# Attention and two expert layers on one core: each engine's instruction order as a written table in place of a list scheduler, with the banded scores' matmul groups of two head pairs joined

## The chip, the cores and the metric

The kernel runs on one core of one Trainium2 chip. Five engines work side by side, each on its own queue of instructions, which it takes in order: PE (TensorE, matmuls, with a separate record PEld for its weight loads), DVE (VectorE), ACT (ScalarE), POOL (GpSimd) and SP (SyncE, which here only issues DMA transfers). An instruction that waits for another engine holds up everything behind it in its own queue. The metric is the device time of one launch in microseconds (us), the median of repeated runs; less is better.

## The reference

Three stages run one after the other. The first is attention over 4 batches, 8 heads, 576 positions of 64 numbers: a full softmax attention over means of 4 neighbouring positions (144 of them), repeated 4 times, plus a banded one in which each position sees only those less than 4 places away. Then come two expert layers over the 2304 tokens of 512 numbers.

```
out_up = np.repeat(sm_attn(q_d, k_d, v_d), 4, axis=2)     # q_d: mean of 4 positions
mask = np.abs(pos[:, None] - pos[None, :]) < 4
scores = np.where(mask, scale * q @ k.T, -1e9)
attn = out_up + softmax(scores) @ v                       # (2304, 512) as x
h = x @ w_in                                              # 512 x 2048
x = (np.maximum(h, 0) + alpha * np.minimum(h, 0)) @ w_out # 2048 x 512
xn = x / np.sqrt(np.mean(x * x) + 1e-6) * rms_g
g = xn @ w_gate                                           # 512 x 1536
out = (g * sigmoid(g) * (xn @ w_val)) @ w_out2            # 1536 x 512
```

## The kernel before

All weights arrive as 64-bit floats and are turned into 32-bit ones on the chip. A piece of a weight lies raw in a tile `wr` (two 32-bit halves to a number, fetched at L1167 or L1177); `decode` (L1186 to L1195) makes it a 32-bit float in a tile `wc` (or `wo`): one ACT pass over the high halves (L1186), for some pieces a second ACT pass over the low ones (L1189) and one DVE pass (L1191), for the others two DVE passes (L1194, L1195). `square` (L1207, tile `sqps`) then lets TensorE multiply each 128-column block with itself, DVE takes the diagonal (L1208), and a sum over all partitions (L415, tile `allps`) gives the scale of that weight. With it every operand is split into a high and a low f16 half (ACT L439, DVE L440), and a product is taken as three f16 matmuls: high by high, high by low, low by high.

The 2304 tokens go through in blocks. **Attention of the first tokens and the decoding of the first weights** fill the start. Queries and keys of a pair of heads are loaded (L819, tile `wo`) and transposed (L868, tile `tps`, copied by ACT at L869 into a tile `T`), then follow the scores of the coarse attention (L891, `sps`), its transposed weights (L919, L920), its product with the values (L928), and the banded attention in chunks: mask (L944, L948), scores (L956, tile `lsps`), exponentials on ACT (L976), transposes (L1000, `ltps`, copied at L1002 into `laT`) and the product with the values (L1012, `lops`). From the output a scaled f16 pair `xt` is made. **First expert layer**: L1432 (`hps`) computes h, ACT and DVE apply the slope (L1436, L1438) and split it (L439, L440) and L1449 (`acc`) multiplies by w_out. Attention of later tokens (DVE and POOL, for some batches TensorE, L545 to L770) lies under these matmuls. **Second expert layer**: L1684 (`pa`, `pb`, `pf`) gate and value products, L1807 (`oacc`) and L1927 (`px`, `py`) the last product, L1932 the copy of the output and L1966 its transfer.

The scores of a pair of heads at L956 and the products at L1012 use a 64-row or 64-column part of TensorE's array, two heads beside each other; most other matmuls use all 128 by 128. A `tile size` below means the part that a matmul uses.

What sets the order: the program records some 9,200 instructions, and at its end `issue_order(tc, nc, groups)` decides in which order each engine takes its own. It is a list scheduler: it knows what each instruction needs, gives each a cost, the waits between engines and a rule for TensorE's two speeds, goes over the program 40 times backward and forward, and keeps the best order that it finds. The table `LEADS` then shifts ranges of instructions by some nanoseconds of priority, and one last pass gives the order, which is nailed down by dependencies between each instruction and the next. Matmuls recorded inside `with together():` form a group that nothing may come between. Each such group holds the 4 matmuls (2 positions by 2 heads) of one head pair:

```python
                for n, h in enumerate(hs):
                    T_ = self.st[h]["T"]
                    with together():
                        for i in range(QC):
                            ...
                                nc.tensor.matmul(ps[j][0:QT, n, i], T_[j * 64:j * 64 + 64, 0, q0:q0 + QT],
```

Of the kernel before, what the change touches and what calls it, by code (L numbers as in the profile page):

```python
# [18 lines left out]
def view(ap, dims, off=0, parts=None):  # L19
# [4 lines left out]
LEADS = (  # L24
# [43 lines left out]
)  # L68


def issue_order(tc, nc, groups, rounds=40):


    insts = [i for i in nc.cur_bb.bb.instructions if i.opcode != "TilePoolBoundary"]
    count = range(len(insts))
    eng = [str(i.engine).split(".")[-1] for i in insts]
    ring, slots = {}, {}
    for t in tc.info.tiles:
        ring.setdefault(t.tag, []).append(t.name)
        slots[t.name] = t.bufs or t.tag_meta.bufs  # L80

    def free(a):
        n = 1
        for _, c in list(a.ap)[1:]:
            n *= c
        return n

    def row(a):
        n = 1
        for d in a.tensor.shape[1:]:  # L90
            n *= d
        return n

    def wide(a):
        return 2 if "16" in str(a.dtype) else 4

    def psum(a):
        return "PSUM" in str(a.tensor.space)

    def span(a):  # L100
        if psum(a):
            return 0, 128, 0, 1 << 20
        p, lo = divmod(a.offset, row(a))
        hi = lo + 1 + sum(abs(s) * (n - 1) for s, n in list(a.ap)[1:])
        return p, p + a.ap[0][1], lo * wide(a), hi * wide(a)

    def meets(x, y):
        return x[0] < y[1] and y[0] < x[1] and x[2] < y[3] and y[2] < x[3]

    def covers(x, y):  # L110
        return x[0] <= y[0] and x[1] >= y[1] and x[2] <= y[2] and x[3] >= y[3]

    def runs(a):
        dims = [list(d) for d in a.ap]
        n, length = 1, 1
        for step, c in reversed(dims):
            if c == 1:
                continue
            if step == length and (n == 1):
                length *= c  # L120
            else:
                n *= c
        return n, length

    def transfer(o, i):
        sides = [[c for _, c in a.ap if c > 1] or [1] for a in (o, i)]
        rings = max(x for x in range(1, 17) if not any(s[0] % x for s in sides))
        n = max(runs(a)[0] for a in (o, i))
        each = 4.0 * min(runs(a)[1] for a in (o, i))
        share = n / 16 * (10.0 + 0.046 * each)  # L130
        return max(share, n / rings * (9.0 + 0.042 * each)), max(share, 600.0)

    def cost(k, ins, outs):
        i, e = insts[k], eng[k]
        if not outs:
            return 60.0
        o, n = outs[0], free(outs[0])
        if e == "SP":
            return transfer(o, ins[0])[0]
        if e == "PE":  # L140
            if wide(ins[0]) == 2:
                return max(25.0, n / 2.4 + 2.5)
            return n * 2 / 2.4 + 3 if i.is_transpose else n * 4 / 2.4 + (128 if n < 64 else 8)
        n = max([n] + [free(a) for a in ins[:1]])
        extra = len([a for a in ins[1:] if free(a) == 1 and n > 1])
        if e == "Activation":
            return (61 if psum(ins[0]) else 103) + n / 1.2 + 93 * (extra + len(outs) - 1)
        if e == "DVE":
            if i.opcode == "Reciprocal":
                return 89 + 6.25 * n  # L150
# [32 lines left out]
    users = {}  # L183
# [136 lines left out]
def kernel(  # L320
# [31 lines left out]
    W = 3  # L352
# [1779 lines left out]
```

## Time and profile before

| | us |
|---|---|
| median of 3 runs | 912.55 (912.38 to 913.46) |
| the profiled execution | 912.48 |
| its span in the trace | 910.8 |
| PE busy | 885.3 (97% of the span) |
| DVE, ACT, POOL busy | 729.8, 570.0, 401.8 |

The profiled execution is within 0.1 us of the median, and its span lies 1.7 us below its own time; what is outside the span is the launch. Busy times are those of the trace and add up to more than the span, since the engines overlap.

### The profile page before, as it was taken

To read this page: it belongs to the slowest core of one execution; us is meant where nothing else is said; L and a number is where in the kernel's file an instruction comes from. 1 tells how busy PE (TensorE), PEld (TensorE's weight loads), DVE (VectorE), ACT (ScalarE), POOL (GpSimd) and SP (SyncE) were. 2 spreads that over 40 slices of the span, in tenths; PEclk is the share of its full clock that TensorE was granted. 3 is DMA by queue.
4 is the path that set the end of the run, shared out by engine and by line. 5 is a ranking of instruction groups with operands and counts; after the bars stand their busy time and mean duration, and the time that the engine had idled before them with its cause. 6 is when DMAs were issued, how large, how long until landed. Compare 5 with 4: busy or idle time off the path is not lost.

```text
span 910.8 us, 16778 instructions
## 1 busy us (share of the span) xinstructions
PE 885.3 (97%) x6394; PEld 592.8 (65%) x6394; DVE 729.8 (80%) x1358; ACT 570.0 (63%) x1332; POOL 401.8 (44%) x314
## 2 busy tenths in 40 slices
PE   7987999999999999999999999999999999999997
PEld 5766877799866666666666656654566644556686
DVE  4789987799898788798789789999899891288772
ACT  5999986255763366765796688983366641356730
POOL 1100204999899999496201233211623100268630
PEclk9998999999999999999999999999999999999999
DMA  9976351174333141340630002220000001100001
GB/s 224 297 261 209 104 182 28 53 234 142 106 89 99 44 95 53 102 139 1 195 87 32 1 1 81 94 70 35 24 13 1 1 1 39 32 1 1 1 19 53
DMA packets 54111, 73.81 MB, mean 81 GB/s; under 512 B 22202, under 2 KB 35918, under 8 KB 54030
## 3 DMA queue, kind: packets, MB, share of 16 engines
q1 hardware_dynamic: 54030, 72.74, 26.7%
q8 instruction: 50, 0.82, 0.4%
q14 instruction: 31, 0.25, 0.1%
HBM read 68.01 MB, written 4.72 MB: 80 GB/s over the span
## 4 chain that ended last, share of the span: by engine, by line
PE 85%; ACT 6%; DVE 3%; DMA 2%; POOL 2%; issue 1%; SPq 0%; DVEq 0%; POOLq 0%; ACTq 0%
PE hps L1432 18%; PE acc L1449 17%; PE pa L1684 14%; PE oacc L1807 10%; PE pf L1684 7%; PE pb L1684 3%; PE px L1927 3%; POOL prod L599 1%; PE py L1927 1%; PE lsps L956 1%; PE tps L868 1%; ACT wr L1186 1%; PE lops L1012 1%; ACT wi L439 1%; PE ltps L1000 1%
## 5 line engine op out<-in xcount | busy, mean ns | idle before, releaser
L1432 PE MATMUL hps<-xt,wi 128*128 128x192 f16 (+1 forms) x1536 | 326.8, 290 | 4.6 <-DVE g L440 3.1
L1449 PE MATMUL acc<-ghl,wo 128*128 128x384 f16 (+1 forms) x960 | 231.0, 310 | 0.0
L1432 PEld LDWEIGHTS <-wi 128*128 128x128 f16 x1536 | 148.6, 100 | 57.1 <-issue 6.5
L1449 PEld LDWEIGHTS <-wo 128*128 128x128 f16 x1344 | 128.4, 98 | 56.7 <-issue 0.8
L545 POOL TENSOR_TENSOR prod<-cq,ckv 128x896 f32<-128x896 f32 x48 | 105.5, 2197 | 41.4 <-DVE hps L1438 35.3
L1684 PEld LDWEIGHTS <-ws 128*128 128x128 f16 x864 | 85.0, 99 | 56.7 <-issue 2.7
L599 POOL TENSOR_TENSOR prod<-ls,ckv 128x896 f32<-128x896 f32 x48 | 91.3, 1903 | 9.8 <-DVE lo L612 6.5
L1807 PE MATMUL oacc<-wi,wo 128*128 128x512 f16 x360 | 95.4, 379 | 0.2 <-ACT ob L1811 0.2
L1684 PEld LDWEIGHTS <-w 128*128 128x128 f16 x648 | 63.8, 99 | 41.6 <-issue 0.5
L1436 ACT ACTIVATE g<-hps 128x384 f32<-128x384 f32 x96 | 47.2, 492 | 61.5 <-PE hps L1432 60.9
L1438 DVE SCALAR_TENSOR_TENSOR hps<-g,oma,hps 128x192 f32<-128x192 f32 (+1 forms) x128 | 65.7, 515 | 18.3 <-ACT g L1436 17.3
L1449 PE MATMUL acc<-g,wo 128*128 128x384 f16 (+1 forms) x384 | 70.3, 286 | 0.1
L1664 POOL TENSOR_TENSOR ws<-w 128x768 f32<-128x768 f16 x12 | 22.1, 1852 | 106.8 <-DVE ws L1571 40.8
L1684 PE MATMUL pa<-x,w 128*128 128x384 f16 x216 | 67.1, 326 | 0.1
L1684 PE MATMUL pb<-x,w 128*128 128x384 f16 x216 | 66.2, 326 | 0.0
L1807 PEld LDWEIGHTS <-wo 128*128 128x128 f16 x360 | 35.3, 98 | 41.8 <-issue 0.5
L439 ACT ACTIVATE ghl<-hps,grp 128x384 f16<-128x384 f32 (+1 forms) x73 | 42.2, 578 | 31.9 <-DVE hps L1438 27.2
L612 DVE TENSOR_REDUCE lo<-prod 128x128 f32<-128x896 f32 x48 | 51.7, 1079 | 9.5 <-POOL prod L599 9.2
L1692 DVE TENSOR_TENSOR sn<-pf,sn 128x384 f32<-128x384 f32 x45 | 24.8, 552 | 42.6 <-ACT sn L1689 36.5
L556 DVE TENSOR_REDUCE ls<-prod 128x14 f32<-128x896 f32 x48 | 51.7, 1078 | 4.6 <-POOL prod L545 4.5
L1689 ACT ACTIVATE sn<-pa 128x384 f32<-128x384 f32 x66 | 31.9, 489 | 32.9 <-PE pa L1684 32.7
L1876 POOL TENSOR_TENSOR wr<-wi 128x512 f32<-128x512 f16 x12 | 15.1, 1261 | 84.1 <-DMA out_dram<-ob 77.5
(365 smaller groups left out, 2122.6 us busy)
## 6 DMA issues: line engine op xcount, KB each, us to landing
wr<-in_moe_w_out_dram SPq DMA_DIRECT2D x18, 512.0 KB
wr<-in_moe_w_in_dram SPq DMA_DIRECT2D x10, 768.0 KB
wr<-in_moe_w_gate_dram SPq DMA_DIRECT2D x8, 768.0 KB
wr<-in_moe_w_val_dram SPq DMA_DIRECT2D x8, 768.0 KB
ckv<-in_k_dram SPq DMA_DIRECT2D x7, 768.0 KB
ckv<-in_v_dram SPq DMA_DIRECT2D x7, 768.0 KB
wr<-in_moe_w_out_dram SPq DMA_DIRECT2D x20, 256.0 KB
out_dram<-ob SPq DMA_DIRECT2D x14, 256.0 KB
```

Source lines behind the costliest of these rows:

```text
L439: nc.scalar.activation(out=hi, in_=src, func=AF.Copy, scale=s)
L545: engs[i].tensor_tensor(out=pr, in0=view(st["q"][:, j, t:t + TP], [[D, TP], [0, ND], [1, D]]), in1=view(st["k"][:, j, t:t + TP], [[D, TP], ...
L556: nc.vector.tensor_reduce(out=st["s"][:, j, t:t + TP], in_=st.pop(("p", i)), axis=AX.X, op=ALU.add)
L599: engs[i].tensor_tensor(out=over(pr, i), in0=view(st["s"][:, j, t:t + TP], [[ND, TP], [1, ND], [0, D]]), in1=view(st["v"][:, j, t:t + TP], ...
L612: nc.vector.tensor_reduce(out=st["o"][:, t:t + TP, j], in_=view(pr, [[ND * D, TP], [ND, D], [1, ND]]), axis=AX.X, op=ALU.add)
L1432: nc.tensor.matmul(ps[:, j], wi[:, f + j, a, kk * 128:(kk + 1) * 128], x[:, b_, kk, c0:c0 + n], start=(i == 0), stop=(i == 3 * KK - 1))
L1436: nc.scalar.activation(out=g, in_=ps, func=AF.Relu, scale=-1.0)
L1438: nc.vector.scalar_tensor_tensor(out=ps[:, j], in0=g[:, j], scalar=oma[:, f + j:f + j + 1], in1=ps[:, j], op0=ALU.mult, op1=ALU.add)
L1449: nc.tensor.matmul(acc[e], wo_f(f)[:, a, e * 128:(e + 1) * 128], hl[:, b_], start=(f == f0 and i == 0), stop=(f == f1 and i == 2))
L1684: nc.tensor.matmul(ps, w[:, a, kk, c:c + 128], x[:, b_, kk], start=(start and n == 0), stop=(n == 3 * K2 - 1), skip_group_check=True)
L1807: nc.tensor.matmul(acc, uhl(f)[:, h, a, tt * 128:(tt + 1) * 128], w[:, b_, f % 3], start=(f == fs[0] and i == 0), stop=(f == fs[-1] and i ...
L1927: nc.tensor.matmul(ps, two(u[g])[:, a, tt * 128:(tt + 1) * 128], w(g, b_), start=(start and g == 0 and i == 0), stop=(g == F2 - 1 and i == 2),
```

## The change

The scheduler, its costs, the `LEADS` and the groups go. In their place stands `ORDER`, a table with one list for each engine; each number is the step from one instruction's place in the program to that of the next. The matmuls, the other work and the transfers are the same 9,181 instructions of data work as before, and only their order on each engine differs. No line is kept that holds the four matmuls of a group together; the table decides it.

```diff
-LEADS = (
-    (8102, 8103, 7000), (776, 777, -500), (3486, 3544, 1500), (7335, 7386, 500), (5591, 5593, -500),
...
-def issue_order(tc, nc, groups, rounds=40):
...
+ORDER = {
+    "Activation": (
+        127, -4, 13, -4, 9, 4, 285, 1, -281, 17, -2, 1, -12, 14, 64, 2, 2, -3, 5, -3, 2, -52, 54, 194, -184, -1, 3,
...
+def issue_order(tc, nc):
+    insts = [i for i in nc.cur_bb.bb.instructions if i.opcode != "TilePoolBoundary"]
...
+    for engine, steps in ORDER.items():
+        k, a = 0, None
+        for step in steps:
+            k += step
+            b = insts[k]
...
+            if a is not None:
+                tc.add_manual_dep(b, a.name, wait if apart(a) else info, reason="issue order")
+            a = b
...
-                    with together():
-                        for i in range(QC):
-                            q0 = W + (c * QC + i) * QT
-                            for j in range(2):
...
+                    for i in range(QC):
+                        q0 = W + (c * QC + i) * QT
+                        for j in range(2):
...
-    issue_order(tc, nc, groups)
+    issue_order(tc, nc)
```

How that moves rows is seen in the order of each engine. A row names the line, the operation, what it writes and reads, its shape, and with x how many stand in a row. After the change lines lie 117 to 121 further down (L956 is L1074, L1432 is L1549, L1186 is L1303).

TensorE, where the banded scores of the third chunk of the first tokens stand among the first layer's matmuls (`T_186` and `T_191` are the transposed queries and keys of two head pairs). Before:

```order
L948 MATMUL lsps<-maskb 96x2x3
L1432 LDWEIGHTS wi
L1432 MATMUL hps<-xt,wi 128x192
L956 MATMUL lsps<-T_186 96x102 x4
L1432 LDWEIGHTS wi
L1432 MATMUL hps<-xt,wi 128x192
L956 MATMUL lsps<-T_191 96x102 x4
L1432 LDWEIGHTS wi
L1432 MATMUL hps<-xt,wi 128x192
L733 MATMUL sps<-qkT 72x144 x4
L1000 MATMUL ltps<-ident,dls 102x96
```

The same place with the change:

```order
L1549 LDWEIGHTS wi
L1549 MATMUL hps<-xt,wi 128x192
L1074 MATMUL lsps<-T_186 96x102 x4
L1074 MATMUL lsps<-T_191 96x102 x4
L855 MATMUL sps<-qkT 72x144 x4
L1118 MATMUL ltps<-ident,dls 102x96
L1549 LDWEIGHTS wi
L1549 MATMUL hps<-xt,wi 128x192
```

The groups of the two head pairs stand next to each other now, and the coarse scores, which use half the array too, behind them, where a matmul of the full array stood between each two before. In the whole program L956 stood in 16 runs of four; now in six runs of eight and four of four. From the first `hps` matmul on, the tile size changes 89 times along TensorE's order, and changed 100 times before.

ACT, from the last copies of `laT` of the first chunk to the first split of w_in (`wi`) and the first slope (`g`). Before:

```order
L1002 ACTIVATE laT<-ltps 102x384
L1186 ACTIVATE wr<-wr 128x768
L439 ACTIVATE xt<-dxs,sc 128x192
L1186 ACTIVATE wr<-wr 128x768
L439 ACTIVATE xt<-dxs,sc 128x192
L1189 ACTIVATE wr<-wr,nhalf 128x768
L1186 ACTIVATE wr<-wr 128x768
L1189 ACTIVATE wr<-wr,nhalf 128x768
L1186 ACTIVATE wr<-wr 128x768
L439 ACTIVATE wi<-wc,swi 128x512 x5
```

With the change:

```order
L1303 ACTIVATE wr<-wr 128x768
L1120 ACTIVATE laT<-ltps 102x384
L1306 ACTIVATE wr<-wr,nhalf 128x768
L1120 ACTIVATE laT<-ltps 102x384
L1303 ACTIVATE wr<-wr 128x768
L562 ACTIVATE xt<-dxs,sc 128x192
L1306 ACTIVATE wr<-wr,nhalf 128x768
L562 ACTIVATE xt<-dxs,sc 128x192
L562 ACTIVATE wi<-wc,swi 128x512 x2
L1303 ACTIVATE wr<-wr 128x768
L562 ACTIVATE wi<-wc,swi 128x512 x3
```

Behind the last `laT` stood four L1186, two L1189 and two `xt` before the first `wi`; now one L1303 (the same line), one L1306 (L1189) and two `xt` do. The others stand ahead of `laT`, but for one L1186 that comes after the first `wi`. Counted from the program's start, 13 of L1186 preceded the first `wi`, and 12 do now; all else ahead of it is the same.

SP, from the program's start, the first loads. Before (the rows of two small vectors are `rows`, a piece of w_in is `wr`):

```order
L819 DMA wo<-in_q_dram 96x6x64
L1167 DMA wr<-in_moe_w_in_dram 128x2x768
L819 DMA wo<-in_q_dram 96x6x64
L819 DMA wo<-in_k_dram 96x6x64
L2031 DMA rows<-in_moe_alpha_dram 16x128
L827 DMA sdv<-in_v_dram 72x2x512
L2031 DMA rows<-in_moe_rms_g_dram 4x128
```

With the change:

```order
L940 DMA wo<-in_q_dram 96x6x64
L2148 DMA rows<-in_moe_alpha_dram 16x128
L940 DMA wo<-in_k_dram 96x6x64
L940 DMA wo<-in_q_dram 96x6x64
L2148 DMA rows<-in_moe_rms_g_dram 4x128
L940 DMA wo<-in_k_dram 96x6x64
L940 DMA wo<-in_q_dram 96x6x64
L1284 DMA wr<-in_moe_w_in_dram 128x2x768
```

The first of these rows is the seventh transfer before and the fifth with the change. The two small rows went from the eleventh and thirteenth place to the sixth and ninth, the first piece of w_in from the eighth to the twelfth, behind two loads of q and k and the two small rows that followed it before. On TensorE the two transposes that read the small rows (L2034, `vecps`) follow their transfers: they stand behind the fifth and the eighth transpose L868 now, and stood behind the seventeenth and the twenty-third.

## Rows read from the trace of the kernel before

**Rows 1.** The page, busy time of each engine (part 1) and the chain (part 4).

```profile
PE 885.3 (97%) x6394; PEld 592.8 (65%) x6394; DVE 729.8 (80%) x1358; ACT 570.0 (63%) x1332; POOL 401.8 (44%) x314
...
PE 85%; ACT 6%; DVE 3%; DMA 2%; POOL 2%; issue 1%; SPq 0%; DVEq 0%; POOLq 0%; ACTq 0%
```

**Rows 2.** Windows: the span cut into stretches, busy time of each engine, granted clock.

```profile
0.00:10.00 10.00, 3.52 (x18) 2.76 (x20) 1.85 (x10) 2.73 (x5) 2.06 (x27) 1.00 0.93 201
10.00:50.00 40.00, 40.00 (x278) 31.04 (x279) 28.89 (x84) 36.35 (x123) 4.84 (x4) 1.00 0.95 267
50.00:60.00 10.00, 8.14 (x67) 6.60 (x66) 9.16 (x25) 8.58 (x14) 0.00 (x0) 1.00 0.72 237
60.00:92.00 32.00, 24.27 (x242) 21.22 (x244) 30.13 (x74) 31.67 (x78) 2.13 (x2) 0.89 0.73 236
92.00:99.00 7.00, 7.00 (x92) 5.66 (x90) 6.57 (x22) 4.79 (x16) 1.97 (x6) 1.00 0.48 132
99.00:905.00 806.00, 802.27 (x5714) 525.54 (x5708) 652.24 (x1145) 485.86 (x1101) 390.82 (x275) 1.00 0.20 62
905.00:911.00 6.00, 0.10 (x1) 0.00 (x0) 1.01 (x3) 0.00 (x0) 0.00 (x0) 0.93 0.24 82
```

**Rows 3.** Chain of waits inside 50 to 93 us: start, length, what.

```profile
57.63 6.66 DMA wr<-in_moe_w_in_dram
...
64.31 0.94 ACT wr L1186
...
91.76 0.55 PE lops L1012 x8
```

**Rows 4.** Waits of ACT, 10 to 92 us: total, times, longest.

```profile
ACT T L869 <- PE tps L868: 1.4, 3, 0.8
ACT aT L920 <- PE atps L919: 1.1, 2, 0.6
ACT laT L1002 <- PE ltps L1000: 0.9, 1, 0.9
ACT wr L1186 <- DMA wr<-in_moe_w_in_dram: 0.8, 2, 0.5
ACT wi L439 <- DVE swi L430: 0.5, 1, 0.5
```

**Rows 5.** Timeline of TensorE: start, length, line, operation, tiles, shapes, count, idle before.

```profile
6.80 1.19 PE L868 MATMUL tps<-ident,wo 96*128 96x96 f32 x6 [3.31 <-DMA wo<-in_q_dram]
8.33 1.22 PE L868 MATMUL tps<-ident,wo 96*128 96x96 f32 x6 [0.34 <-ACT T L869]
...
33.28 1.55 PE L1012 MATMUL lops<-laT,vw 102*64 102x96 f32 x16
34.78 0.76 PE L891 MATMUL sps<-qkp 64*72 64x144 f32 x4
...
50.60 0.91 PE L1012 MATMUL lops<-laT,vw 102*64 102x96 f32 x8
51.44 0.40 PE L1000 MATMUL ltps<-ident,dls 96*102 96x96 f32 x1
```

**Rows 6.** The same view, runs of the first layer's matmuls, and the banded scores among them.

```profile
60.80 2.42 PE L1432 MATMUL hps<-xt,wi 128*128 128x192 f16 x14 [0.40 <-DVE wi L440]
...
64.40 1.81 PE L1432 MATMUL hps<-xt,wi 128*128 128x192 f16 x20
...
94.81 0.24 PE L1432 MATMUL hps<-xt,wi 128*128 128x192 f16 x1
94.98 0.60 PE L956 MATMUL lsps<-T 64*96 64x102 f32 x8
95.51 0.26 PE L1432 MATMUL hps<-xt,wi 128*128 128x192 f16 x1
```

**Rows 7.** Waits of PE, 99 to 905 us.

```profile
PE pa L1684 <- ACT sn L1689: 1.6, 3, 0.8
PE atps L761 <- ACT dd L752: 1.0, 1, 1.0
```

More of the change, by code (lines that the diff above doesn't have):

```diff
@@ L1 @@
-import heapq
 from collections import deque
-from contextlib import ExitStack, contextmanager
+from contextlib import ExitStack
 import concourse.bass as bass
@@ L312, in issue_order, with apart @@
+ORDER = {
+    "Activation": (
[51 rows of a table added]
+    ),
+    "DVE": (
[60 rows of a table added]
+    ),
[255 rows of a table added]
+    ),
+    "Pool": (
[13 rows of a table added]
+    ),
[12 rows of a table added]
+    ),
+}
+def issue_order(tc, nc):
+    insts = [i for i in nc.cur_bb.bb.instructions if i.opcode != "TilePoolBoundary"]
     info, wait = [mybir.DependencyInfo(c, mybir.DependencyReason.DATA)
                   for c in (mybir.DependencyClass.NoSync, mybir.DependencyClass.Sync)]
-    for q in best[1].values():
-        for a, b in zip(q, q[1:]):
-            tc.add_manual_dep(insts[b], insts[a].name, wait if apart[a] else info, reason="issue order")
+    def apart(i):
+        outs = [a.bass_ap for a in i.outs if hasattr(a, "bass_ap")]
+        return str(i.engine).endswith("Pool") and outs and outs[0].tensor.name.split("_")[0] in ("prod", "sd", "qkp", "dd")
+    placed = 0
+    for engine, steps in ORDER.items():
[3 more added lines that the diff above has]
+            b = insts[k]
+            assert str(b.engine).split(".")[-1] == engine
+            if a is not None:
+                tc.add_manual_dep(b, a.name, wait if apart(a) else info, reason="issue order")
+            a = b
+            placed += 1
+    assert placed == len(insts)
@@ L357 @@
     P_X, P_W, P_H = 13, 14, 15
-    groups = []
-    @contextmanager
-    def together():
-        n = len(nc.cur_bb.bb.instructions)
-        yield
-        groups.append([i.name for i in nc.cur_bb.bb.instructions[n:]])
     P_N, P_U, P_G, P_O = 8, 38, 13, 13
@@ L729, in smm @@
             ps = [ps_t.tile([128, 2, SD], F32, tag="at", name="sps") for j in range(2)]
-            with together():
-                for a in range(2):
-                    for j in range(2):
-                        nc.tensor.matmul(
-                            ps[j][0:SH, a], t[j * 64:j * 64 + 64, 0, a * SH:(a + 1) * SH],
-                            t[j * 64:j * 64 + 64, 1, :], start=True, stop=True)
+            for a in range(2):
+                for j in range(2):
+                    nc.tensor.matmul(
+                        ps[j][0:SH, a], t[j * 64:j * 64 + 64, 0, a * SH:(a + 1) * SH],
+                        t[j * 64:j * 64 + 64, 1, :], start=True, stop=True)
             a_ = st["buf"][:, 0:4 * SD].rearrange("p (j a k) -> p j a k", j=2, a=2)
@@ L769, in avm @@
             ps = ps_t.tile([128, SD], F32, tag="at", name="avps")
-            with together():
-                for kh in range(2):
-                    for j in range(2):
-                        nc.tensor.matmul(ps[j * 64:j * 64 + 64, :], st["pv"][:, kh, j],
-                                         st["aT"][:, j, kh * SD:(kh + 1) * SD], start=(kh == 0), stop=(kh == 1))
+            for kh in range(2):
+                for j in range(2):
+                    nc.tensor.matmul(ps[j * 64:j * 64 + 64, :], st["pv"][:, kh, j],
+                                     st["aT"][:, j, kh * SD:(kh + 1) * SD], start=(kh == 0), stop=(kh == 1))
             nc.scalar.activation(out=outd_t[b][:, h, :], in_=ps, func=AF.Copy)
@@ L887, in smm @@
                 ps = [pool_of(self.smp[j]).tile([128, 2, SD], F32, tag=self.smp[j], name="sps") for j in range(2)]
-                with together():
-                    for a in range(2):
-                        for j in range(2):
-                            nc.tensor.matmul(
-                                ps[j][0:SH, a], t[j * 64:j * 64 + 64, 0, a * SH:(a + 1) * SH],
-                                t[j * 64:j * 64 + 64, 1, :], start=True, stop=True)
+                for a in range(2):
+                    for j in range(2):
+                        nc.tensor.matmul(
+                            ps[j][0:SH, a], t[j * 64:j * 64 + 64, 0, a * SH:(a + 1) * SH],
+                            t[j * 64:j * 64 + 64, 1, :], start=True, stop=True)
                 m = att.tile([SH, 2, 2], F32, tag=f"dm{h % 2}", name="dm")
@@ L924, in avm @@
                 ps = ps_t.tile([128, SD], F32, tag="at", name="avps")
-                with together():
-                    for kh in range(2):
-                        for j in range(2):
-                            nc.tensor.matmul(ps[j * 64:j * 64 + 64, :], st["pv"][:, j, kh],
-                                             st["aT"][:, j, kh * SD:(kh + 1) * SD], start=(kh == 0), stop=(kh == 1))
+                for kh in range(2):
+                    for j in range(2):
+                        nc.tensor.matmul(ps[j * 64:j * 64 + 64, :], st["pv"][:, j, kh],
+                                         st["aT"][:, j, kh * SD:(kh + 1) * SD], start=(kh == 0), stop=(kh == 1))
                 if h == 0:
@@ L951, in s1 @@
                     T_ = self.st[h]["T"]
-                    with together():
-                        for i in range(QC):
-                            q0 = W + (c * QC + i) * QT
-                            for j in range(2):
-                                nc.tensor.matmul(ps[j][0:QT, n, i], T_[j * 64:j * 64 + 64, 0, q0:q0 + QT],
-                                                 T_[j * 64:j * 64 + 64, 1, q0 - W:q0 + QT + W],
-                                                 start=False, stop=(n == 1 and i == QC - 1))
+                    for i in range(QC):
+                        q0 = W + (c * QC + i) * QT
+                        for j in range(2):
+                            nc.tensor.matmul(ps[j][0:QT, n, i], T_[j * 64:j * 64 + 64, 0, q0:q0 + QT],
+                                             T_[j * 64:j * 64 + 64, 1, q0 - W:q0 + QT + W],
+                                             start=False, stop=(n == 1 and i == QC - 1))
                 m = att.tile([QT, 2, QC, 2], F32, tag=f"lm{h0}", name="dlm")
@@ L1008, in s4 @@
                     ps = pool_of(banks[n]).tile([128, QC, QT], F32, tag=banks[n], name="lops")
-                    with together():
-                        for i in range(QC):
-                            for j in range(2):
-                                nc.tensor.matmul(ps[j * 64:j * 64 + 64, i], st["vw"][:, c * QC + i, j],
-                                                 ls["t"][n][:, i, j], start=True, stop=True)
+                    for i in range(QC):
+                        for j in range(2):
+                            nc.tensor.matmul(ps[j * 64:j * 64 + 64, i], st["vw"][:, c * QC + i, j],
+                                             ls["t"][n][:, i, j], start=True, stop=True)
                     tag = ("ob", "xs", "ra", "rb")[h]
```

218 lines of the change are left out of this document (removed), and 432 rows, old and new, of tables (LEADS, ORDER).

## Prediction

> **What bounds the kernel now.** I read the page first: TensorE is busy for 885.3 of 910.8 us and holds 85% of the chain [rows 1]. An order can shorten the rest, or make TensorE's own work shorter, and nothing else. The windows then say where the rest lies [rows 2]. TensorE is idle for 6.5 us of the first 10 (10.00 less 3.52), for none of the 40 to 50 us, for 1.9 us from 50 to 60, for 7.7 from 60 to 92, for none from 92 to 99, for 3.7 from 99 to 905 (806.00 less 802.27) and for 5.9 in the tail; together 25.7. So there are three regimes. Up to 92 us the start, in which ACT is the fullest engine: 36.35 of 40, 8.58 of 10, 31.67 of 32 us. From 92 to 905 us TensorE, full to within 3.7 us. Then the copy and the transfer of the output.
>
> The chain inside the start shows the hand-over [rows 3]: from a transfer of w_in, 57.63 us, through ACT's decoding from 64.31 us on to TensorE's `lops` at 91.76 us, after which TensorE doesn't wait any more for ACT. Whatever ACT's own work is, it must be done before; only ACT's idle time ahead of that point can be won there. The list of ACT's waits from 10 to 92 us gives 1.4 us for `T`, 1.1 for `aT`, 0.9 for `laT`, 0.8 for transfers and 0.5 for the scale `swi` [rows 4], 4.7 together.
>
> TensorE runs the start at two speeds. Eight small `lops` matmuls took from 50.60 to 51.44 us, 0.84, and 0.55 at 91.76 us with the last one's end in it [rows 3, 5]; fourteen `hps` at 60.80 us took 2.42 us (0.17 each) and twenty at 64.40 us 1.81 us (0.09 each) [rows 6]. That is the step from 1.2 to 2.4 GHz, in the middle of the first layer's first matmuls. The granted clock is 0.89 on the mean from 60 to 92 us, so some 22% of that stretch, 7 us, is at the lower level again; from 99 us on it is 1.00 [rows 2].
>
> **The change, term by term.** All sums stand against the profiled execution, 912.48 us; the median is 0.07 above it, which I leave out.
>
> *The hand-over from ACT to TensorE.* The same work stands ahead of the first layer, but for one decode (L1186, 0.94 us in [rows 3]) that moves behind the first `wi`; it must still be done before 91 us, so I count nothing for it. What moves the hand-over is ACT's idle time. Two decodes that stood behind the last `laT` now stand ahead of it, so ACT has something to do where it waited 0.9 us for `ltps`: -0.9. The decodes on which the scale hangs are earlier, so the wait of 0.5 us for `swi` goes: -0.5. The loads of q and k pass the first 768 KB piece of w_in, so the transposes of the second pair of heads and their `T` copies can come earlier; that wait is 1.4 us, and ACT used part of the time before for the decode that is now later, so I take half: -0.7. Against it, the two small rows' transposes stand ahead of the first transposes of k. TensorE takes its queue in order, so these k transposes and the `T` copies behind them wait for two more transfers. The price isn't in the trace; from below it is nothing, from above 1.5 us, the distance between the first q and the first k transposes (6.80 and 8.33 us, [rows 5]), and I take 0.5, nearer to nothing since these rows are small and were issued early: +0.5. Sum -1.6, with the bounds -4.7 (all of ACT's idle time goes) and +1.5 (nothing goes, and the small rows cost all they can).
>
> *Joined groups and fewer changes of tile size.* In the saturated part every saved nanosecond of TensorE counts. From `hps` at 94.81 to the scores at 94.98 us lie 0.17 us, where `hps` to `hps` takes 0.09 [rows 6]: 0.08 to get in. What it costs to get out I read from the products L1012: sixteen in one run took 34.78 less 33.28, 1.50 us, and eight took 0.84 [rows 5], so two runs of eight 1.68, 0.18 more at the lower clock; half of that, 0.09, at the upper. A join saves one way in and one out, 0.17 us. Four of the six joins lie in the part that TensorE bounds: -0.7. All 11 changes of tile size that go after the first `hps` would give 11 x 0.085 = 0.9. I take the latter, -0.9, since the coarse scores and others moved together too; the bounds are nothing (the engine behind a group was waited for anyway) and -1.0.
>
> *The waits from 99 to 905 us.* There are 3.7 us to win and no limit to what may be lost. The two largest are `pa` for ACT's `sn`, 1.6 us in three waits, and `atps` for `dd`, 1.0 in one [rows 7]. The new order takes the matmuls of the second layer in shorter turns: L1684 in 201 runs where there were 120, L1807 in 118 for 67. Shorter turns put more other work between a matmul and what it needs, and also more products of different tiles in flight. I count 0, with -3.7 and +4 as bounds, the latter five waits like the longest `pa` one (0.8).
>
> *The tail.* The last matmuls, the two copies of the output and its transfer keep their order; the 5.9 us stay.
>
> **Sum:** 912.48 - 1.6 - 0.9 = 910.0 us.
>
> **Rivals.** *The clock rises earlier or falls less (faster).* In the new order the squares before the first `hps` stand together more purely, with the small products L1012 behind them, and TensorE's waits between 60 and 92 us, 7.7 us, may lie elsewhere. If the 7 us at the lower level were run at the upper, the work in them would take half, 3.5 us less; against it, the lower level lies in a stretch that ACT bounds, so TensorE's speed there only counts where ACT waits for it. With the forecast's terms that gives 912.48 - 2.5 - 3.5 = 906.5 us. The Trainium skill (TensorE: Matmul & The Clock Gate, Part 1 and Part 4) says that activity releases the lower rate and that transposes on TensorE don't count as activity in the same way. The trace agrees with the first half only in part, since TensorE was busy for 40 of 40 us from 10 to 50 and still took 0.84 us for eight products at 50.60.
>
> *The order makes new waits in the saturated part (slower).* A table that is right for one set of durations has no slack where a duration is another: TensorE waits at the head of its queue, with all matmuls behind it. The place is the second layer, `pa` on ACT's `sn`, where the three waits of before are 0.5 us each [rows 7] and turns are shorter now. It decides from 4.3 us of new waits on (2.5 for the terms above and 1.8 for the bound of what can be measured), eight or nine such waits among the 201 turns; with ten, 5.3 us, the time is 915.3. Against it: ACT is busy for 485.86 of 806 us there and DVE for 652.24 [rows 2], so both have room.
>
> *The order does what it says and nothing is won.* ACT's idle time moves to other waits, since the same decodes and transfers must be done before 91 us, and the tile changes lie under other latencies. Then it is 912 us, some tenths either way. For it speaks that ACT is busy for 31.67 of 32 us from 60 on, whatever the order.
>
> **How the numbers follow.** The forecast (two terms, 908.5 to 910.7) gets 0.37, the earlier clock 0.20, no gain 0.25, new waits 0.18. I predict the likeliest, 910.0 us. A measurement of this kernel tells about 0.2%, 1.8 us, from no change: faster by more than that are the first two, 0.57, same 0.25, slower 0.18. The range drops a tenth at either end: below, the clock's case with the larger bound of the first term on top of it (905.5), above, new waits of about 4.5 us with no gain elsewhere half kept (915.0).
>
> **What would show each step.** First term: the chain hands over to TensorE before 91 us, and ACT's waits from 10 to 92 us come to less than 4.7, with none for `swi` and `laT`; the first `hps` lies near 58 us. If the small rows cost, the first k transposes start later than 8.33 us. Second: the joined scores in one row of sixteen matmul passes with 1.1 us or less, and TensorE's busy time from 99 on smaller by under 1 us. Third: the waits of TensorE after 99 us near 3.7. Tail: 5.9 us. The prediction is wrong if the waits after 99 us are over 6, if the stretch to 92 us ends more than 4 us earlier, or if the granted clock before 92 us is another.

## The result, and the profile after

The changed kernel is slower by half a percent: 917.91 us (median of 6 runs, 916.20 to 921.90) against 912.87 us of the kernel before on the same chip, a ratio of 1.0051 with a 95% interval of 1.0027 to 1.0075. The forecast was 910.0 us, and its range ended at 915.0.

The page of the profiled execution, whose span is 917.2 us, with the busy times and the chain by engine that answer to [rows 1]:

```profile
PE 882.2 (96%) x6394; PEld 590.5 (64%) x6394; DVE 729.3 (80%) x1358; ACT 567.6 (62%) x1332; POOL 404.6 (44%) x314
...
PE 76%; ACT 6%; POOL 6%; DVE 5%; DMA 3%; SPq 2%; issue 1%; DVEq 0%; POOLq 0%; ACTq 0%
```

TensorE is busy for 3 us less, and the span is 6.4 us longer. GpSimd's share of the chain rose from 2% to 6%. The windows tell where, in the stretches of [rows 2] from 10 us on; the columns are as there:

```profile
10.00:50.00 40.00, 33.38 (x229) 25.75 (x228) 26.19 (x71) 31.59 (x102) 5.76 (x8) 1.00 0.92 247
50.00:60.00 10.00, 7.19 (x55) 5.83 (x56) 5.37 (x15) 6.41 (x26) 2.71 (x1) 1.00 0.81 255
60.00:92.00 32.00, 22.38 (x220) 19.10 (x218) 29.87 (x70) 31.03 (x53) 0.00 (x0) 0.88 0.70 221
92.00:99.00 7.00, 6.85 (x73) 6.48 (x73) 6.14 (x24) 5.83 (x25) 1.69 (x2) 0.81 0.59 161
99.00:905.00 806.00, 802.07 (x5747) 525.28 (x5745) 656.15 (x1166) 490.20 (x1128) 392.60 (x283) 1.00 0.21 62
```

From 99 to 905 us nothing changed: 3.9 us of idle TensorE, 3.7 before. The loss is in the start. TensorE was busy for all 40 us from 10 to 50 and is now for 33.38; ACT, which bounds the start, for 31.59 instead of 36.35 there, and for 6.41 instead of 8.58 from 50 to 60. The first layer's first matmul shows what the start lost; before, and with the change:

```profile
59.91 0.50 PE L1432 MATMUL hps<-xt,wi 128*128 128x192 f16 x2 [0.82 <-ACT wi L439]
...
66.54 0.26 PE L1549 MATMUL hps<-xt,wi 128*128 128x192 f16 x1 [1.26 <-ACT wi L562]
```

It comes 6.6 us later, and the span is 6.4 us longer. The list of ACT's waits from 10 to 92 us, which answers to [rows 4] (5.2 us over the whole list then, with two small rows that [rows 4] leaves out, 12.7 now), names three places:

```profile
ACT aT L1040 <- PE atps L1039: 4.8, 2, 3.6
ACT T L990 <- PE tps L989: 3.7, 5, 1.7
ACT wr L1303 <- DMA wr<-in_moe_w_in_dram: 2.6, 2, 2.2
```

The first is followed back with GpSimd's timeline. `dd` is its multiplication of the coarse attention's weights by the reciprocals of their sums; the four of the first tokens are the same work, 72 by 576 numbers each. The third and the fourth:

```profile
41.94 1.14 POOL L1029 TENSOR_TENSOR dd<-dd,dsum 72x576 f32<-72x576 f32 x1 [8.06 <-DVE dsum L1028]
47.94 4.76 POOL L1029 TENSOR_TENSOR dd<-dd,dsum 72x576 f32<-72x576 f32 x1 [4.86 <-ACT dls L1094]
```

The first three take 1.14 us each, the fourth 4.76. In VectorE's timeline over the same time stands a chain of six instructions without a gap, from 48.16 us until 51.70: four of decodes, a split and a short reciprocal.

```profile
48.16 0.55 DVE L1311 TENSOR_SCALAR wc<-wr 128x768 int32<-128x768 int32 x1
48.62 1.82 DVE L1312 SCALAR_TENSOR_TENSOR wc<-wr,wc 128x768 int32<-128x768 int32 x2
50.36 0.41 DVE L563 SCALAR_TENSOR_TENSOR xt<-dxs,sc,xt 128x192 f16<-128x192 f32 x1
50.69 0.15 DVE L558 RECIPROCAL sc<-sc 128x1 f32<-128x1 f32 x1
50.77 0.94 DVE L1308 SCALAR_TENSOR_TENSOR wo<-wr 128x768 int32<-128x768 int32 x1
```

The `dd` ends 1.0 us after the last of them, 52.70 us, about as long as it takes alone. TensorE's transposes `atps` wait for it, and ACT's copy `aT` waits 3.6 us behind that (above):

```profile
PE atps L1039 <- POOL dd L1029: 3.5, 1, 3.5
```

The Trainium skill (SBUF — State Buffer, Who interferes with whom) says that VectorE and GpSimd share a pair of ports as an exclusive lock, which a VectorE instruction with two inputs from the SBUF, or in a two-port mode, holds for its whole length, and that who issues first decides. The trace agrees on the first: 3.6 us of standstill beside that chain. It goes beyond it, since GpSimd was kept out for a chain of six instructions and not for one, and it differs on who comes first, as the last section tells.

The second and third wait belong to transfers, at least in their largest parts. The first decode of w_in begins at 14.77 us (10.50 before), after ACT has waited 2.2 us. On TensorE the transposes of a k piece begin at 25.78 us after 3.23 us of idle time; the last part of that piece landed at 25.69 us.

### The profile page after: what moved, and what is told of

The parts are those of the page before. It is cut to its first block, busy times and chain, and to the rows that moved or that the text cites. A ratio compares the mean times of both kernels' runs of the same rounds, so it can differ in the third digit from the quotient of the medians.

```text
span 917.2 us, 16746 instructions
## 1 busy us (share of the span) xinstructions
PE 882.2 (96%) x6394; PEld 590.5 (64%) x6394; DVE 729.3 (80%) x1358; ACT 567.6 (62%) x1332; POOL 404.6 (44%) x314
## 4 chain that ended last, share of the span: by engine, by line
PE 76%; ACT 6%; POOL 6%; DVE 5%; DMA 3%; SPq 2%; issue 1%; DVEq 0%; POOLq 0%; ACTq 0%
PE acc L1566 16%; PE hps L1549 15%; PE pa L1801 14%; PE oacc L1924 9%; PE pf L1801 7%; PE pb L1801 4%; PE px L2044 3%; POOL prod L722 3%; POOL prod L668 2%; DMA sdv<-in_v_dram 1%; PE py L2044 1%; DMA wr<-in_moe_w_out_dram 1%; ACT wr L1303 1%; SPq L940 1%; DVE lo L735 1%
## 5 line engine op out<-in xcount | busy, mean ns | idle before, releaser
L1549 PE MATMUL hps<-xt,wi 128*128 128x192 f16 (+1 forms) x1536 | 326.9, 289 | 7.2 <-DVE g L563 4.2
L1566 PE MATMUL acc<-ghl,wo 128*128 128x384 f16 (+1 forms) x960 | 228.4, 310 | 0.0
L1549 PEld LDWEIGHTS <-wi 128*128 128x128 f16 x1536 | 147.2, 100 | 58.2 <-issue 4.4
L1924 PE MATMUL oacc<-wi,wo 128*128 128x512 f16 x360 | 98.0, 379 | 0.7 <-ACT ob L1928 0.7
L1566 PE MATMUL acc<-g,wo 128*128 128x384 f16 (+1 forms) x384 | 74.7, 286 | 0.1
L1801 PE MATMUL pa<-x,w 128*128 128x384 f16 x216 | 64.6, 326 | 0.0
L1781 POOL TENSOR_TENSOR wo<-w 128x768 f32<-128x768 f16 x17 | 29.7, 1749 | 48.8 <-DVE ws L1688 15.6
```

The costliest lines, as they stand in the source:

```text
L1549: nc.tensor.matmul(ps[:, j], wi[:, f + j, a, kk * 128:(kk + 1) * 128], x[:, b_, kk, c0:c0 + n], start=(i == 0), stop=(i == 3 * KK - 1))
L1566: nc.tensor.matmul(acc[e], wo_f(f)[:, a, e * 128:(e + 1) * 128], hl[:, b_], start=(f == f0 and i == 0), stop=(f == f1 and i == 2))
L1781: nc.gpsimd.tensor_tensor(out=tmp(t), in0=w[:, 0], in1=w[:, 1], op=ALU.add)
L1801: nc.tensor.matmul(ps, w[:, a, kk, c:c + 128], x[:, b_, kk], start=(start and n == 0), stop=(n == 3 * K2 - 1), skip_group_check=True)
L1924: nc.tensor.matmul(acc, uhl(f)[:, h, a, tt * 128:(tt + 1) * 128], w[:, b_, f % 3], start=(f == fs[0] and i == 0), stop=(f == fs[-1] and i ...
```

## The experiments

Fifteen kernels ran. The kernel before ran beside each on the same chip, with medians of 914.06 us (e1 to e4), 914.62 (e5 to e8), 913.33 (e9 to e12) and 913.51 (e13 to e15); each ratio is against it. The ratio is an estimate of its own with its interval, and not the quotient of the two medians (for e11 that would be 0.9973).

| | kernel | median us | ratio, 95% interval |
|---|---|---|---|
| e1 | new order to 100 us, old behind | 919.44 | 1.0059 (1.0038 to 1.0080) |
| e2 | old to 93 us, new behind | 913.18 | 0.9989 (0.9968 to 1.0010) |
| e3 | new, with the old order of transfers | 948.54 | 1.0373 (1.0338 to 1.0409) |
| e4 | old, with the new order of transfers | 942.92 | 1.0315 (1.0277 to 1.0353) |
| e5 | new, `dd` freed | 913.63 | 0.9983 (0.9963 to 1.0002) |
| e6 | old to 35 us, new behind | 915.26 | 1.0011 (0.9991 to 1.0030) |
| e7 | as e6, `dd` freed | 913.04 | 0.9983 (0.9962 to 1.0004) |
| e8 | new to 36 us, old behind | 916.13 | 1.0016 (0.9990 to 1.0043) |
| e9 | the changed kernel again | 915.80 | 1.0030 (1.0012 to 1.0048) |
| e10 | as e5 | 913.35 | 0.9996 (0.9978 to 1.0014) |
| e11 | as e7 | 910.87 | 0.9985 (0.9966 to 1.0004) |
| e12 | `dd` freed one instruction later | 912.88 | 0.9991 (0.9974 to 1.0008) |
| e13 | a wait that frees nothing | 913.93 | 0.9994 (0.9974 to 1.0013) |
| e14 | as e5 | 912.50 | 0.9999 (0.9975 to 1.0023) |
| e15 | the changed kernel again | 915.84 | 1.0019 (1.0002 to 1.0036) |

**Which part of the program: e1, e2.** The tables, with 9,179 entries in all, are cut at one place in the program. P holds the first 508 matmuls in the new order (e1; 523 in the old, e2) and all that they need:

```diff
-ORDER[e] = new[e]
+ORDER[e] = [k for k in new[e] if k in P] + [k for k in old[e] if k not in P]   # e1
+ORDER[e] = [k for k in old[e] if k in P] + [k for k in new[e] if k not in P]   # e2
```

> The first 943 instructions (all that TensorE's first 508 matmuls need, to about 100 us) in the new order, all behind them in the order of before. Theory 'start': the whole loss lies ahead of 100 us, so this is as slow as the change, 916 to 919 us, 3.5 to 6 above before. Rival 'rest': the shorter turns of the saturated part cost it; then this is 912 to 913.5. The trace of the changed kernel speaks for the start (TensorE's waits after 99 us come to 3.6 us, and were 3.7).

> The mirror image: the first 983 instructions in the order of before, all behind them in the new one. Theory 'start': within 1 us of before, 911.5 to 913.5, a little faster if the joined scores and the fewer changes of tile size give what the forecast gave them (0.9 us less the part already in the start, about 0.5 us). Rival 'rest': 916 or more.

The new start alone is as slow as the change; with the old start and the new rest the kernel is not slower than before. The loss is in the start, and the rival of the saturated part falls: by e2's interval the new rest costs 0.1%, 0.9 us, at most.

**The order of transfers: e3, e4.** Only SyncE's list is exchanged:

```diff
-ORDER["SP"] = new["SP"]
+ORDER["SP"] = old["SP"]   # e3; e4 the other way round
```

> The new order on TensorE, VectorE, ScalarE and GpSimd, but SyncE issues its transfers in the order of before. Theory 'transfers': the late landing of v (27.22 us for the piece that landed at 21.07 before) and of w_in starves the start, so with the old order of transfers most of the loss goes, 912 to 914. Rival 'compute order': the loss comes from the order on the other engines (GpSimd's multiplication held up by VectorE, 4.76 us for 1.14), so it stays near 917, or is worse since the two orders don't fit each other.

> The order of before on all engines but SyncE, which issues in the new order. Theory 'transfers': 915 to 918. Rival 'compute order': within 1 us of before, unless an engine stands waiting for a transfer that the new order issues later (the first piece of w_in, four places later, some 4 us).

Both are some 30 us slower, which no theory had. In e3 TensorE stands 4.6 us at the transpose of the small rows, which now come late, and 8.2 us at `hps` behind `ghl` later on. An order of transfers fits one order of compute; exchanged whole, it tells nothing on the cause.

**The held multiplication and the first loads: e5 to e8.** The freed kernels have one more dependency; 363 is the fourth `dd`, 476 the shift of VectorE's decode (L1311 above):

```diff
+    tc.add_manual_dep(insts[476], insts[363].name, wait, reason="issue order")
     assert placed == len(insts)
```

e6 to e8 are cut as e1 and e2 are, at 35 us.

> The new order with one added wait: VectorE's decode that stood beside GpSimd's last multiplication dd (4.76 us in the changed kernel and in the kernel with the new start, 1.14 elsewhere) starts when it is done. Theory 'shared access': VectorE's five decodes without a pause from 48.16 to 51.7 us hold GpSimd up; then this dd takes 1.14 us, the wait of TensorE's atps (3.5 us) and that of ScalarE's aT (3.6) go, VectorE loses about 1.1, and the time falls by 2 to 3, to 915 to 916. Rival 'hidden': ScalarE has the same work to do before the first layer can run freely, and what is won there is lost before 95 us; no change, 917 to 919.

> The order of before up to 35 us (304 instructions: first loads, first transposes, first attention), the new one behind. Theory 'first loads': the small rows ahead of the k transposes and the later landing of w_in and v cost 1.3 to 2.7 us by 45 us in the two kernels with the new start, so this is 1.5 to 2.5 below the change, 915 to 916.5, and the fourth dd is still held up. Rival 'later part alone': all of it lies behind 35 us, 917 to 919.

> Both: the order of before up to 35 us, the new one behind, and the fourth dd freed by the added wait. If both theories hold, and add, the loss is gone: 912 to 914. If the later part of the start (35 to 95 us) loses by something else as well, 914.5 to 916. If neither holds, 917.

> The mirror: the new order up to 36 us (254 instructions), that of before behind. Theory 'first loads': 1.5 to 2.5 above before, no dd above 1.5 us. Rival 'later part alone': within 1 us of before.

With one added wait the new order is at 0.9983, where it was at 1.0051 (measured apart from it; e9 and e10 below repeat this side by side). In e6 the fourth `dd` is held too (4.70 us), in e7 it takes 1.14, and the ratio falls from 1.0011 to 0.9983. What the first 35 us cost stays open: by the medians e8 lies 1.5 us above the kernel before, where the theory 'first loads' begins, and e6 only 0.6, but the intervals of both hold 1, and e5 and e7 are alike. In every kernel that has the new order at this place and no added wait (the change, e1, e3, e6, e9, e15) the fourth `dd` is held, with 4.70 to 4.77 us. The expectation of e5 counts five decodes; the chain has four instructions of decodes, with the split and the reciprocal six in all.

**Again, with more rounds: e9 to e12.** e12 is e5 with the wait on the next instruction of VectorE, so that the shift runs beside the `dd`:

```diff
-    tc.add_manual_dep(insts[476], insts[363].name, wait, reason="issue order")
+    tc.add_manual_dep(insts[474], insts[363].name, wait, reason="issue order")
```

> The changed kernel itself beside the freed ones on the same chip. 0.4 to 0.6% above before, if the first measurement of it holds; the fourth dd takes 4.7 to 4.8 us again, since it does not hang on when transfers land.

> The new order with VectorE's decode waiting for the fourth dd, again, with more rounds. Theory 'shared access': 0.5 to 0.7% below the changed kernel on this chip, and 0.1 to 0.2% below before (the trace of the first run had 1.4 us less of TensorE's lost time than before). Rival 'chance of the first runs': within 0.2% of the changed kernel.

> The old order up to 35 us, the new one behind, the fourth dd freed. If the first loads of the new order cost something, this is below the freed new order by 0.1 to 0.3%; if they cost nothing, the two are the same within 0.1%. In both cases below before by 0.1 to 0.4%.

> As the freed new order, but VectorE waits for the dd one instruction later: the shift of the decode (one input from the SBUF, 0.55 us) runs beside it, and the two ORs (two inputs each, 0.9 us each) wait. Theory 'any of the decode's instructions holds GpSimd': dd takes 1.6 to 1.8 us (the 0.2 before the shift, its 0.55, and the rest). Theory 'only instructions with two inputs do': dd takes 1.14 us. The time is that of the freed order within 0.1% either way.

The change costs 0.30% here, less than was expected, and the freed order nothing; 2.5 us lie between their medians. e11 has the lowest median of all, and was 0.9985 where e7, the same kernel, was 0.9983; each interval just reaches 1. Put together, each weighted by its interval, they give 0.16% below the kernel before, give or take 0.14: an estimate by which the old first 35 us with the new rest and a free `dd` do win about 1.5 us. e12 gave 1.14 us for the `dd`, as the theory of two inputs had it, but for another reason, which VectorE's row shows:

```profile
44.35 1.34 DVE L1314 TENSOR_SCALAR wc<-wr 128x768 int32<-128x768 int32 x1
```

The shift takes 1.34 us where it took 0.55. It begins 0.22 us after the `dd` (44.13 us) and ends 0.4 after it. Here GpSimd held VectorE. So the shift with its one input is in the contest too, and the question is who wins.

**Held or landed late: e13 to e15.** A last doubt was left: in the profiles of the change and of e9 the first transfers landed late, and in those of e5, e10 and e12 they did not, so the freed kernels could owe their gain to that. e13 has the wait of e5 on the third `dd` (360), which is done long before:

```diff
-    tc.add_manual_dep(insts[476], insts[363].name, wait, reason="issue order")
+    tc.add_manual_dep(insts[476], insts[360].name, wait, reason="issue order")
```

> The new order with a wait added at the same instruction as in the freed kernel, but for GpSimd's third dd, which is done some 5 us before; nothing is freed. Theory 'held dd': the fourth dd takes 4.76 us and the time is that of the changed kernel, 0.3 to 0.5% above before and above the freed one. Rival 'landing': the gain of the freed kernel came from earlier landings; then w_in lands near 12.3 us here, the dd still takes 4.76, and the time is that of the freed kernel, within 0.1% of before.

> The freed kernel beside it: -0.2 to 0.0% against before in both theories, dd 1.14 us.

> The changed kernel beside it: 0.3 to 0.5% above before in both theories, dd 4.76 us.

e13 came out otherwise than both theories: the wait, though long fulfilled, freed the `dd`. First ACT's first decode in e13, then VectorE and GpSimd in it:

```profile
14.63 0.89 ACT L1306 ACTIVATE wr<-wr 128x768 f32<-128x768 f32 x1 [2.15 <-DMA wr<-in_moe_w_in_dram]
...
48.16 1.34 DVE L1314 TENSOR_SCALAR wc<-wr 128x768 int32<-128x768 int32 x1
...
47.94 1.14 POOL L1032 TENSOR_TENSOR dd<-dd,dsum 72x576 f32<-72x576 f32 x1 [4.86 <-ACT dls L1097]
```

The two begin at the very times of the changed kernel, 47.94 and 48.16 us, and the lock goes to the other one. And this profile has the late landing, while e15, the changed kernel again, has the early one, its first decode and its `dd`:

```profile
12.50 0.89 ACT L1305 ACTIVATE wr<-wr 128x768 f32<-128x768 f32 x1
...
44.11 4.77 POOL L1031 TENSOR_TENSOR dd<-dd,dsum 72x576 f32<-72x576 f32 x1 [4.86 <-ACT dls L1096]
```

e14 came out as expected, and e15 at 0.19%, less than expected. So landing and lock vary apart from each other, and the spans of the eight profiles that have the new order throughout fill a table of two by two:

| span, us | first decode of w_in at 12.3 to 13.0 us | at 14.6 to 14.8 us |
|---|---|---|
| `dd` 1.14 us | e5 908.9, e10 911.0, e12 909.9, e14 910.6; mean 910.1 | e13 914.2 |
| `dd` 4.76 us | e15 912.6 | the change 917.2, e9 917.2 |

The held `dd` costs 2.5 us in the left column (912.6 less 910.1) and 3.0 in the right. The late landing costs 4.1 in the upper row and 4.6 in the lower. Three of the four cells hold one or two profiles, and the four spans in the first differ by 2.1 us. The first `hps` matmul fills the same table with less scatter: it begins at 58.9 to 59.5 us in e5, e10, e12 and e14, at 63.0 in e13, at 62.7 in e15, and at 66.5 and 66.3 in the change and e9. That is 3.5 us for the held `dd` in either column.

The runs give the held `dd` the same size: between the medians on one chip lie 2.5 us (e9 less e10) and 3.3 (e15 less e14), between the means 2.6 and 2.3, each give or take 1.6. One thing these kernels can't part: wherever the wait was added, the `dd` was free too. That it is the `dd` and not the wait itself that counts is read from the traces, in which TensorE's 3.5 us for `atps` are there with the held `dd` and gone without it.

## Why the prediction was wrong

**The step that failed is the hand-over from ACT to TensorE.** Its text said that what moves the hand-over is ACT's idle time, took 2.1 us off it and put 0.5 on. ACT's waits from 10 to 92 us came to 12.7 us, where 5.2 had been, and the first `hps` began at 66.54 us, where the text had said near 58. What was missing is a resource that stands in none of the queues: the access that VectorE and GpSimd share. The new order puts the fourth `dd` beside a chain of VectorE's decodes; before, two reductions that read PSUM (L962, from 39.98 us) stood beside it, and it took 1.14 us. Shown by e9 against e10, e15 against e14 and the table above: some 2.5 to 3 us. None of the rivals had it; the slower one placed its waits in the second layer. The trace of the kernel before held a small case that could have been read, its second `dd` beside its fourth:

```profile
25.21 1.42 POOL L909 TENSOR_TENSOR dd<-dd,dsum 72x576 f32<-72x576 f32 x1 [5.87 <-ACT dls L991]
...
39.69 1.14 POOL L909 TENSOR_TENSOR dd<-dd,dsum 72x576 f32<-72x576 f32 x1 [4.64 <-DVE dsum L908]
```

When the second began, VectorE was in an addition of two parts of a tile in the SBUF (L883, 24.96 to 25.61 us), and it took 0.28 us more than the others.

Piece by piece. The wait for `swi` (0.5) is gone, as said. So is that for `laT` (0.9): it stood before the last copy of the first chunk, and both copies there run without a wait in the changed kernel and in e10. A wait of the same size, 0.9 us, has come up before a later chunk's `laT`, past 91 us. For `T` half of 1.4 us was to go; it has grown instead, to 3.2 in e10 and 4.0 in e15, and `aT` was not in the sum. The small rows ahead of the k transposes were put at 0.5 us between 0 and 1.5; the second copy of k into `T` runs from 10.60 to 11.01 us, where the pair had ended by 9.99, so they cost about 1.0, with a `rowps` matmul that now stands there too, inside the bounds. So even without the held `dd` the list of ACT's waits is longer than before, 7.2 to 8.2 us (e5, e10, e12, e14) for 5.2, and yet the first `hps` begins 0.4 to 1.0 us earlier than before. The sum of ACT's waits was not a good measure of the hand-over; what made up for them was not followed up. The whole sum, without the held `dd`, gives a kernel at 0.9983 to 0.9999 (e5, e10, e14), where the forecast of -2.5 us was to be 0.9973. All three intervals reach 1, and those of e10 and e14 begin above 0.9973: a gain of the freed order is not shown, and it is smaller than forecast.

**Late transfers** were not in the sum at all. They come and go between profiles of one kernel (e9 and e15); they add some 4 us to a profile in which they happen, and explain, as far as the profiles go, why the first profile of the change lost 6.4 us where the held `dd` costs 3. All three profiles of the table that have them, like the other five there, have the new first loads, with which the first decode of w_in begins at 12.3 us or later; in the five with the old ones (the kernel before, e2, e6, e7, e11) it begins at 10.4 to 10.8. Whether the new order makes them likelier is not shown.

**Joined groups.** The mechanism was right and the size too small. A joined run in the changed kernel, with a matmul of the full array behind it:

```profile
110.53 0.95 PE L1074 MATMUL lsps<-T 64*96 64x102 f32 x16
111.41 0.26 PE L1549 MATMUL hps<-xt,wi 128*128 128x192 f16 x1
```

Sixteen passes and the way out take 0.88 us from start to start, where two runs of eight took 0.53 each with theirs, and one way in of 0.08 more [rows 6]; a join saves 0.26 us, where the forecast had 0.17. In the time it is not to be seen apart: e2, which has all joins of the saturated part, is at 0.9989 with an interval of 0.4%.

**Waits from 99 to 905 us**: counted at no change, and so it was: TensorE's idle time is 3.9 us where it was 3.7. The rival of new waits there is refuted by e2. **Clock**: 0.88 from 60 to 92 us and 0.81 from 92 to 99, before 0.89 and 1.00. The earlier clock did not come, and the lower level in the second stretch (7 us at 0.81, so 2.7 us of half rate) fell differently in every profile; e2 and e11 show mean clocks of 0.990 and 0.993 and no loss. **Tail**: the last matmul ends at 912.07, 5.15 us before the span's end; before it was 5.68 (the 5.9 of the text count to 911 us, past the end of the span). What the text lists as making it wrong (waits after 99 us, an earlier end of the start, another clock) did not come up; a later end of the start is not in that list.

## What to carry to other kernels

When an order is changed, look at what runs beside what and not only at what waits for what: list the instructions of VectorE and GpSimd that will overlap and read from the trace what an overlapped one of each kind has cost. Here a chain of VectorE instructions on SBUF data without a gap kept GpSimd out for its whole length, and one wait at its first or second instruction was enough to let it in. A single profile of a start that hangs on transfers can be 4 us off by chance; compare several before a cause is named.

## What the runs showed of the hardware

The winner of the shared access is not simply the one that starts first in the records, where the rule of the Trainium skill cited above goes by who issues first. In the changed kernel, in e12 and in e13 the `dd` starts 0.22 us before VectorE's shift. In the changed kernel it then waits for six instructions, 3.6 us; in e12 and e13 it holds the shift for 0.8 us (1.34 less 0.55). What differs is a wait on GpSimd: on the shift itself in e13, on the instruction behind it in e12. Why a wait that is already fulfilled turns the contest stays open; what was not tried is a wait on another engine, or another instruction in the chain.

The first piece of w_in, issued at 6.4 us behind the same transfers, had landed by 11.9 us in e15 and at 14.6 in e9, two profiles of one kernel. Why is open.
